# A gated mix of a long convolution and a dense block on one core: first weights and six first-layer blocks moved into the FFT phase, one record buffer for the power tables

## The chip, the core and the metric

The kernel runs on one core of one Trainium2 chip. The metric is device time in microseconds for one execution; the median of 11 runs is given. A page of the profile and a trace come from one further execution, and its own time stands beside its span below. TensorE multiplies matrices, VectorE (DVE in the profile) and ScalarE (ACT) do elementwise work, GpSimd (POOL) mostly issues DMAs here, and SyncE (SP) only issues DMAs.

## The reference

Sequence length L = 2048, width D = 448, state N = 256, hidden width F = 1792, all in bfloat16. The forward part is a gate between two blocks:

```
g = sigmoid((x * gate_w).sum(-1))
dt = exp(log_dt); dB = dt * (B_re + 1j B_im); C = C_re + 1j C_im
P[d,n,l] = exp(dt * (A_re + 1j A_im) * l)          # l rounded to bfloat16
K[d,l]   = real(sum_n C[d,n] P[d,n,l] dB[d,n])
a = irfft(rfft(u, 2L) * rfft(K, 2L))[:L] + u * Dskip
b = relu(x2 @ w1 + b1)**2 @ w2 + b2
out = g * a + (1 - g) * b
```

The function returns `out` and the gradients to all inputs but the dense block's input (14 of them) for a given `grad_out`. Both are computed in one program.

## The kernel before, in words

A Python program writes out the instructions, and a planner puts them in a fixed order for each engine: it works with its own costs, starts each instruction where its operands and engine are free, and keeps the program's order as the priority. `tc.issue_after(x)` tells it not to issue something ahead of x. Each engine then runs its list strictly in order, so an instruction that waits holds up everything behind it on that engine. The same holds for the DMA issues, which stand in the lists of SP, ScalarE and GpSimd. On-chip buffers are tiles with a tag (U16, R32, F17, P14, K28, S25, D16, ...): a new tile of a tag takes the memory of the old one, and what writes it waits for the last readers of that part of the memory. The profile shows a tile by the letter of its tag: R is R32, F is F17, P is P14, S is S25, U is U16, D is D16, K is K28.

**The FFT phase.** A convolution of length 4096 is done as two-stage FFTs on TensorE (`fwd1`, L230; `fwd2`, L258), through scratch in memory. `fwd1` on u and on DA (grad_out times g) fills gd; `spectrum(w, q)` (L664) reads a quarter q of gd back, runs `fwd2`, and stores the spectrum. The products of the two spectra (`cprod`, L281) and the first inverse stage (`inv1p`, L295, evacuated by L207, L208 and L217) give hd[0], which holds the gradient DK to the convolution kernel before its last stage; the eight stores of hd are issued by ScalarE (L299). `transposed` (L493, copies L496, stores L498) puts u and DB (grad_out times 1 - g) into memory in transposed form, as UT_d and DBT_d, in four blocks of 512 positions each, by way of three buffers in tag S25.

**The power tables.** The convolution kernel needs powers of exp(dt A). They are kept in 14 chunks of 32 channels each. `powers(gr)` (L625 to L655) makes the records of four chunks (the fourth group has two): the seeds (L640 to L644), then 11 levels. A level copies the current powers into the record (L648, ScalarE), squares them (L651, ScalarE), multiplies real by imaginary part (L652, VectorE) and subtracts the squares (L653, VectorE); the result is the next level's input. Then GpSimd stores the record of 1,920 KB (960 for the last) to rec_d (L655). There are two sets of buffers, `psets` (L609): a record buffer, two buffers that the powers alternate between (`cur`), and one for the squares. Set 0 has its record in tag F17 (F), its powers in R32 and its squares in W0, which is tag P14; set 1 has all three in R32 (R). The groups alternate between the sets. The program calls `powers(0)` after spectrum(0, 0), `powers(1)` after spectrum(1, 0), and `powers(2)` and `powers(3)` in the first two rounds of the loop over q.

**DK's way through memory.** hd[0] is loaded in four quarters, of which two go to tag D16 (D) and two to tag P14 (P); each is loaded in two halves, one issued by ScalarE and one by SP (`load_hs`, L322). TensorE sums them with constants (L721), ScalarE copies the sums (L725 to L727), they are stored to dk_d on both the SP and the GpSimd queue (L734), and come back in another form (L741, L743) to the top of tag K28 (DK). The weights w1 of the first dense layer are loaded by SP into tag U16 (L705, L708) and two UT blocks by GpSimd (`load_ut`, L576) into tag S25 in the same stretch. The loads of w2 (tag D16, L1037) are held back with `issue_after(lry1)` until the load of the second part of chunk 1's record (`load_ry`).

**The chunk loop.** For each chunk c, `load_rx` and `load_ry` bring the record (L806, L810), `expand_x` and `expand_y` (ScalarE, L815 to L822) spread it into tag F17, VectorE starts the tables (`seeds_x`, L802) and doubles them (`build_x`, L781 to L785; `build_y`, L792 to L795). TensorE makes the kernel rows from them (`kgen`, L852; `k_out`, L860) and transposes them (L878, L890; the transposes are copied by L879 and L891, or done by DMA, L898). For the gradient, `dk_chunk` (L903, L904) prepares DK, `back_z` multiplies (L921, copied by L925 on ScalarE), `back_p` multiplies by the tables on VectorE (L941) and sums on TensorE (L950). The back part of chunk c - 1 runs beside the build of chunk c.

**The dense block, woven into the chunk loop.** `hidden(lb, jp)` (L592, L595, then relu L597 and square L599 or L602 on ScalarE, and a store to rT_d, L603) makes two of the 14 first-layer tiles for block lb of 512 positions. It uses the UT block in S25, w1 in U16, writes the squares to S25 and the relu to a small ring. The six blocks hidden(0, 0) to hidden(0, 5) are called behind round c = 0 of the chunk loop (L1012 to L1014), with the PSUM banks X and S. All other dense work is called behind the loop, and the planner fills it into the loop's gaps: `project` (L1029) with the second weights, transposes of the weights (L1053, L1064), `row_block` (L1092 to L1105) for the gradient to the hidden layer.

**After the loop.** The finished kernel K is stored (L866), loaded in positions (`X<-k_d`, L1121 and L1124), and goes through `fwd1` (L230) and the FFTs for the output and the gradient to u. The weight gradients (L1178) follow from rT_d and dhT_d, which are loaded in rows (L1167).

Of the kernel before, what the change touches and what calls it, by code (L numbers as in the profile page):

```python
# [19 lines left out]
P = 128  # L20
L, D, N, F = 2048, 448, 256, 1792
LT = L // P
FT = F // P
DT = 4
# [9 lines left out]
RS = 1920  # L34
# [303 lines left out]
def kernel(ctx, tc, A_u, A_A_re, A_A_im, A_B_re, A_B_im, A_C_re, A_C_im, A_log_dt, A_Dskip,  # L338
# [3 lines left out]
    nc = tc.nc  # L342
    V, S, G_, T_ = nc.vector, nc.scalar, nc.gpsimd, nc.tensor
# [26 lines left out]
    K = Ker(tc, pool, psum)  # L370
# [66 lines left out]
    RA = K.t("R32", [P, 16384])  # L437
# [43 lines left out]
    SB = K.t("S25", [P, 12800])  # L481
# [93 lines left out]
    def load_ut(lb):  # L575
        G_.dma_start(UTb[lb % 2].rearrange("p a l -> p (a l)"), bass.AP(tensor=UT_d, offset=lb * P * 2048, ap=[[2048, P], [1, 2048]]))  # L576
# [29 lines left out]


    Fp = K.t("F17", [P, 8704])
    psets = [(Fp[:, 0:4 * RS], RA[:, 14336:16384], W0[:, 3584:4608]), (RA[:, 0:4 * RS], RA[:, 7680:9728], RA[:, 9728:10752])]  # L609

    def fields(r):

# [12 lines left out]
    def powers(gr):  # L625
        nch = min(4, NCH - 4 * gr)
        cs_ = slice(4 * gr, 4 * gr + nch)
        n = nch * W2
        rb, cb, qb = psets[gr % 2]
        R = rb.rearrange("p (c r) -> p c r", c=4)[:, 0:nch]  # L630
        xs, ys, lx, ly = fields(R)
        cur = [cb[:, 1024 * i:1024 * i + 1024].bitcast(fp32) for i in range(2)]
        sqr = qb.bitcast(fp32)

        def halves(ap):
            return ap[:, 0:2 * n].rearrange("p (t c w) -> p t c w", t=2, w=W2)
        lam = Lam[:, :, cs_]
        va = cur[1][:, 0:2 * n].rearrange("p (c t w) -> p c t w", t=2, w=W2)
        ua = cur[0][:, 0:2 * n].rearrange("p (c t w) -> p c t w", t=2, w=W2)
        S.copy(xs[:, :, :, :, 1], Wt[:, cs_])  # L640
        V.tensor_tensor(out=ua, in0=Wt[:, cs_], in1=lam[:, 0].unsqueeze(2).to_broadcast([P, nch, 2, W2]), op=ALU.mult)
        V.tensor_tensor(out=va, in0=Wt[:, cs_], in1=lam[:, 1].unsqueeze(2).to_broadcast([P, nch, 2, W2]), op=ALU.mult)
        V.tensor_tensor(out=xs[:, :, 0, :, 3], in0=ua[:, :, 0], in1=va[:, :, 1], op=ALU.subtract)
        V.tensor_tensor(out=xs[:, :, 1, :, 3], in0=ua[:, :, 1], in1=va[:, :, 0], op=ALU.add)  # L644
        x, y = lam, halves(cur[0])
        for k in range(NLEV):
            dst = xs[..., 2] if k == 0 else ys[..., 1] if k == 2 else lx[..., (1, 8, 9, 10).index(k)] if k in (1, 8, 9, 10) else ly[..., k - 3]
            S.copy(dst.rearrange("p c t w -> p t c w"), x)  # L648
            if k < NLEV - 1:
                sq = halves(sqr)  # L650
                S.activation(sq, x, ACT.Square)  # L651
                V.scalar_tensor_tensor(out=y[:, 1], in0=x[:, 0], scalar=2.0, in1=x[:, 1], op0=ALU.mult, op1=ALU.mult)  # L652
                V.tensor_tensor(out=y[:, 0], in0=sq[:, 0], in1=sq[:, 1], op=ALU.subtract)  # L653
                x, y = y, halves(cur[1 - k % 2])
        G_.dma_start(bass.AP(tensor=rec_d, offset=4 * gr * P * RS, ap=[[RS, P], [P * RS, nch], [1, RS]]), R)  # L655


    spw = K.t("K28", [P, 4, 4, 2, D])
    Pct = K.t("U16", [P, 8192])
    K.MIn = Pct[:, 7168:7296]  # L660
    K.st_more = [SB[:, 1792 * i:1792 * i + 1792].rearrange("p (a d) -> p a d", d=D) for i in range(2)]
    S.mul(K.MIn, K.MI[:, P:2 * P], -1.0)
    prd = [b.rearrange("p (i a d) -> p i a d", i=4, d=D) for b in (Pct[:, 0:3584], Pct[:, 3584:7168], RA[:, 10752:14336])]

    def spectrum(w, q):
        sp = spw[:, 2 * (q % 2) + w]
# [11 lines left out]
    for q in range(4):  # L678
        if q < 3:
            if q > 0:  # L680
                spectrum(0, q + 1)
            ls1 = spectrum(1, q + 1) or ls1
        for h in range(2):
            pr = prd[(2 * q + h) % 3]
            K.cprod(pr, spw[:, 2 * (q % 2) + 1], spw[:, 2 * (q % 2)], h)
            K.inv1p(pr, 2 * q + h, hd[0])
        if q == 0:
            with tc.issue_after(f10.ins):
                transposed(DB, DBT_d, (S.copy, V.tensor_copy))
        if q < 2:  # L690
            powers(q + 2)
    with tc.issue_after(ls1.ins):
        nc.sync.dma_start(bass.AP(tensor=DB_d, offset=0, ap=[[LT * D, P], [1, LT * D]]), flat(DB))
        load_const("Ew", nc.sync)
        NW2 = 32 * len(ekeys) - 4096
        Ew2 = SB[:, 10752:10752 + NW2]
        nc.sync.dma_start(Ew2, nc.inline_tensor(cs["Ew2"].astype(ml_dtypes.bfloat16), name="c_Ew2").ap())
    hsD, hsP = K.t("D16", [P, 8192]), K.t("P14", [P, 7168])
    hss = [b[:, 3584 * i:3584 * i + 3584].rearrange("p (g x d) -> p g x d", g=4, x=2) for b in (hsD, hsP) for i in range(2)]
    for q in range(4):  # L700
        lhs = K.load_hs(hd[0], q, hss[q], True)
    w1v = K.t("U16", [P, 8192])
    w1w = w1v[:, 0:7168].rearrange("p (a f) -> p a f", a=DT)
    with tc.issue_after(lhs.ins):
        nc.sync.dma_start(w1w[:, 0:3], bass.AP(tensor=B_w1.tensor, offset=B_w1.offset, ap=[[F, P], [P * F, 3], [1, F]]))  # L705
    for h in range(2):
        with tc.issue_after(lhs.ins):
            nc.sync.dma_start(w1w[64 * h:64 * h + 64, 3], bass.AP(tensor=B_w1.tensor, offset=B_w1.offset + 384 * F, ap=[[F, 64], [1, F]]))  # L708
    KB = K.t("K28", [P, 14336])
    DK = KB[:, 0:VA * D].rearrange("p (a d) -> p a d", d=D)  # L710
    G_.memset(KB[:, 12 * D:VA * D].bitcast(fp32), 0.0)
# [25 lines left out]
    for cpy in range(2):  # L737
        qe = (nc.sync, G_)[cpy]
        with tc.issue_after(ldk[cpy].ins):
            for (a0, na, r0, st_, _) in pieces:  # L740
                qe.dma_start(DK[64 * cpy:64 * cpy + 64, a0:a0 + na].rearrange("p a d -> p (a d)"),  # L741
                             bass.AP(tensor=dk_d, offset=r0 * D, ap=[[na * D, 64], [1, na * D]]))
            qe.dma_start(DK[64 * cpy:64 * cpy + 1, 12], bass.AP(tensor=dk_d, offset=768 * D, ap=[[D, 1], [1, D]]))  # L743

# [4 lines left out]
    XWs = [XB[:, 4096 * k:4096 * k + 4096].rearrange("p (t w a r) -> p t w a r", t=2, w=W2, a=NA) for k in range(2)]  # L749
    for k in range(2):  # L750
        mx = G_.memset(XB[:, 4096 * k:4096 * k + 4096].bitcast(fp32).rearrange("p (x n) -> p x n", n=NA)[:, :, VA:NA], 0.0)
    with tc.issue_after(mx.ins):
        load_ut(0)
        load_ut(1)
    Fv = K.t("F17", [P, 8704])
    Vt = Fv[:, 0:4096]
    PRY = Fv[:, 4096:5376].rearrange("p (l w t d) -> p l w t d", l=5, t=2, d=2)
# [215 lines left out]
    for c in range(NCH + 1):  # L973
# [15 lines left out]
        for half in range(2):  # L989
# [19 lines left out]
            ap = None  # L1009
            if c > 0:  # L1010
                ap = back_p(c - 1, XTs[c - 1][half], (z01, z23)[half], (2 * half, 2 * half + 1), ay if c < NCH else None)
        if c == 0:  # L1012
            for jp in range(6):
                hidden(0, jp, NT[4:6], [w1v[:, 7168:8192], Fv[:, 2048:3072], Fv[:, 3072:4096]])  # L1014

    ring = [w1v[:, 7168:8192], Fv[:, 2048:3072], Fv[:, 3072:4096], P2[:, 0:1024], P2[:, 1024:2048]]
    ni = 0
# [15 lines left out]

    w2v = K.t("D16", [P, 8192])
    w2n = w2v[:, 0:FT * D].rearrange("p (j d) -> p j d", d=D)
    with tc.issue_after(lry1.ins):
        G_.dma_start(w2n, bass.AP(tensor=B_w2.tensor, offset=B_w2.offset, ap=[[D, P], [P * D, FT], [1, D]]))  # L1037
    hidden(0, 6, NT[0:3], ring)
    for lb in range(4):
# [433 lines left out]
```

## Time and profile before

| what | value |
|---|---|
| median of 11 runs | 927.29 us (920.89 to 939.61) |
| the profiled execution | 917.96 us, span of the trace 916.2 us |
| TensorE busy (matmul) | 705.4 us, 77% |
| VectorE busy | 671.4 us, 73% |
| ScalarE busy | 577.5 us, 63% |
| GpSimd busy | 198.5 us, 22% |
| mean granted TensorE clock | 0.838 of full speed |
| DMA | 184.97 MB, mean 202 GB/s |

The span covers the instructions of one execution; all positions in us are counted from its start. A busy share is an average over the whole span, and the stages differ: from 60 to 90 us VectorE is busy 29.32 of 30 us, from 182 to 200 us TensorE is busy 2.67 of 18 us, from 228 to 252 us VectorE is busy 8.94 of 24 us and ScalarE 22.63.

How to read a row of the timeline: the start and the duration in us, the engine, the line of the kernel, the operation, the tile written and the tile read with their shapes, how many instructions were merged, and in square brackets how long the engine was idle before it and what ended that. SPq, ACTq and POOLq are the engines' own instruction queues; a DMA issued from there is not done when the row ends. A list of DMA issues gives the KB of one and the median us from issue to landing. In the chain of waits a row is only a start, a duration and what it was. A row by stretch gives the busy times of PE, PEld, DVE, ACT and POOL in that stretch with the number of instructions, then the TensorE clock, the DMA share and GB/s.

### The profile page before, as it was taken

How to read it: one execution, taken by the hardware profiler on the slowest of the kernel's cores; microseconds unless marked ns; L12 is line 12 of the kernel's file. 1: busy time of each engine (PE TensorE's matmuls, PEld its weight loads, DVE VectorE, ACT ScalarE, POOL GpSimd, SP SyncE). 2: the span in 40 equal slices, each digit the busy share in tenths (PEclk: the TensorE clock that was granted, in tenths of full speed). 3: DMA queues.
4: the chain of work that ended last, by engine and by line, in shares of the span. 5: the costliest groups of instructions: out<-in, count | busy, mean ns of one | idle time of the engine just before them, and what ended most of it. 6: DMA issues, size and time to landing. Idle time of an engine off the chain costs nothing.

```text
span 916.2 us, 18868 instructions
## 1 busy us (share of the span) xinstructions
PE 705.4 (77%) x7585; PEld 334.6 (37%) x7585; DVE 671.4 (73%) x1164; ACT 577.5 (63%) x915; POOL 198.5 (22%) x347
## 2 busy tenths in 40 slices
PE   3637676636978988788888988889859949989895
PEld 1212222224344443344444443444323315543352
DVE  4649968697399999999987899963418959759200
ACT  4537757716997879788687666565516634654543
POOL 2321000113202112121202311223213013354220
PEclk9755555658879899999967999999979879998998
DMA  8997395897536765457652965649999988789861
GB/s 202 350 186 269 121 363 235 305 307 221 138 69 130 151 141 126 101 120 161 152 128 68 235 157 158 143 141 258 322 410 270 303 259 248 219 228 276 187 163 54
DMA packets 169823, 184.97 MB, mean 202 GB/s; under 512 B 100531, under 2 KB 146904, under 8 KB 168808
## 3 DMA queue, kind: packets, MB, share of 16 engines
q1 hardware_dynamic: 118710, 81.48, 37.1%
q0 software_dynamic: 21344, 67.46, 22.4%
q10 hardware_dynamic: 29682, 34.84, 12.0%
q8 instruction: 59, 0.97, 0.4%
q14 instruction: 28, 0.23, 0.1%
HBM read 88.22 MB, written 73.13 MB: 176 GB/s over the span
## 4 chain that ended last, share of the span: by engine, by line
DVE 31%; PE 26%; ACT 14%; DMA 14%; issue 8%; SPq 3%; POOL 2%; ACTq 1%; POOLq 0%; DVEq 0%
PE psF L1178 5%; DVE F L793 4%; DVE P L941 4%; DMA hd<-st 3%; SPq L459 2%; PE psN L1029 2%; DVE Y L795 2%; DVE K L795 2%; DVE X L781 2%; DVE K L792 2%; DVE Y L792 2%; DVE F L782 2%; PE psN L1178 2%; DVE X L785 2%; DMA S<-rT_d 1%
## 5 line engine op out<-in xcount | busy, mean ns | idle before, releaser
L941 DVE TENSOR_TENSOR P<-R 128x2048 bf16<-128x2048 bf16 x42 | 49.5, 1218 | 25.2 <-ACT R L925 21.8
L925 ACT CAST R<-psF 128x1024 bf16<-128x1024 f32 x56 | 57.3, 1024 | 11.3 <-PE psF L921 11.2
L1178 PEld LDWEIGHTS <-S 128*128 128x128 bf16 x448 | 41.9, 100 | 53.6 <-issue 11.5
L1029 PE MATMUL psN<-D,S 128*128 128x448 bf16 x208 | 50.6, 374 | 6.3 <-ACT S L599 6.3
L1178 PE MATMUL psF<-U,S 128*128 128x448 bf16 x224 | 50.2, 370 | 2.9 <-ACT S L1173 2.8
L592 PE MATMUL psN<-S,U 128*128 128x512 bf16 x132 | 41.0, 429 | 8.2 <-ACT F L597 4.8
L921 PE MATMUL psF<-R,S 64*32 64x256 bf16 (+1 forms) x1344 | 36.8, 288 | 9.4 <-DMA R<-Y 3.6
L208 DVE CAST K<-psN 128x448 bf16<-128x448 f32 x36 | 22.0, 621 | 28.3 <-PE psN L258 28.1
L1092 PE MATMUL psN<-S,U 128*128 128x512 bf16 x126 | 36.2, 405 | 6.9 <-ACT D L1097 6.9
L781 DVE TENSOR_TENSOR X<-X,F 128x512 bf16<-128x512 bf16 (+1 forms) x70 | 37.5, 535 | 4.9 <-ACT F L815 3.1
L1105 POOL DMA_DIRECT2D dhT_d<-D x28 | 20.2, 721 | 91.4 <-DVE D L1104 91.0
L793 DVE TENSOR_TENSOR F<-K,F 128x2048 bf16<-128x2048 bf16 (+3 forms) x42 | 35.9, 854 | 3.7 <-ACT F L822 3.7
L258 PEld LDWEIGHTS <-M 128*64 128x64 bf16 x192 | 14.4, 133 | 64.7 <-issue 61.9
L792 DVE TENSOR_TENSOR K<-K,F 128x2048 bf16<-128x2048 bf16 (+3 forms) x42 | 36.4, 866 | 1.7
L782 DVE TENSOR_TENSOR F<-X,F 128x512 bf16<-128x512 bf16 (+1 forms) x70 | 37.0, 528 | 0.7 <-ACT F L816 0.2
L792 DVE TENSOR_TENSOR Y<-Y,F 128x2048 bf16<-128x2048 bf16 (+3 forms) x42 | 36.3, 864 | 1.6
L795 DVE TENSOR_TENSOR K<-K,F 128x2048 bf16<-128x2048 bf16 (+3 forms) x42 | 36.4, 866 | 1.3
L795 DVE TENSOR_TENSOR Y<-Y,F 128x2048 bf16<-128x2048 bf16 (+3 forms) x42 | 36.3, 865 | 1.3
L793 DVE TENSOR_TENSOR F<-Y,F 128x2048 bf16<-128x2048 bf16 (+3 forms) x42 | 35.9, 854 | 0.3 <-ACT F L822 0.3
L1029 PE MATMUL psN<-S,D 128*128 128x448 bf16 x168 | 35.7, 361 | 0.0
L921 PEld LDWEIGHTS <-S 64*16 64x16 bf16 (+1 forms) x1792 | 21.9, 89 | 33.3 <-issue 26.5
L891 ACT COPY M<-psX 128x1024 bf16<-128x1024 bf16 x26 | 26.5, 1019 | 11.7 <-PE psX L890 11.5
(407 smaller groups left out, 1939.2 us busy)
## 6 DMA issues: line engine op xcount, KB each, us to landing
sp<-K ACTq DMA_DIRECT2D x8, 896.0 KB, 4.1
hd<-st ACTq DMA_DIRECT2D x16, 448.0 KB, 5.1
dhT_d<-D POOLq DMA_DIRECT2D x28, 256.0 KB, 5.2
R<-sp SPq DMA_DIRECT2D x8, 896.0 KB, 25.6
S<-rT_d POOLq DMA_DIRECT2D x14, 512.0 KB, 6.6
R<-hd SPq DMA_DIRECT2D x16, 448.0 KB, 8.6
rec_d<-F POOLq DMA_DIRECT2D x2, 1920.0 KB, 8.0
Y<-gd SPq DMA_DIRECT2D x4, 896.0 KB, 10.6
```

Of the source, the lines that this page charges most:

```text
L592: T_.matmul(ps[:], lhsT=w1w[:, dt, j * P:j * P + P], rhs=ub[:, dt], start=(dt == 0), stop=False, skip_group_check=True)
L781: V.tensor_tensor(out=hi4, in0=lo, in1=bcast_dims(pr, [0, (None, n), 1]), op=ALU.mult)
L782: V.tensor_tensor(out=Vv.rearrange("p (x a r) -> p x a r", x=2 * W2, r=2), in0=lo, in1=bcast_dims(pi, [0, (None, n), 1]), op=ALU.mult)
L792: V.tensor_tensor(out=hi, in0=lo, in1=bcast_dims(pr, [0, (None, n // 2), 1]), op=ALU.mult)
L793: V.tensor_tensor(out=Vv.rearrange("p (x a q) -> p x a q", x=rows, q=2), in0=lo, in1=bcast_dims(pi, [0, (None, n // 2), 1]), op=ALU.mult)
L795: return V.tensor_tensor(out=T4[:, :, :, n:2 * n], in0=T4[:, :, :, n:2 * n], in1=V4, op=ALU.add)
L921: T_.matmul(psz[32 * ii:32 * ii + m, t, 256 * s:256 * s + 256], lhsT=DKc[64 * t:64 * t + 64, s, g, 2 * ii:2 * ii + 1 + par].rearrange("p i ...
L925: S.copy(zb[:, :, :, gg].rearrange("p s t n -> p t s n"), psz[:].rearrange("p t (s n) -> p t s n", s=2))
L941: lastp = V.tensor_tensor(out=pr.rearrange("p s t g n -> p s t (g n)"), in0=zv, in1=(xb if r == 0 else rev_dim(xb, 2)), op=ALU.mult)
L1029: lastm = T_.matmul(ps[:, 0:D], lhsT=hblk[j][:, P * tt:P * tt + P], rhs=ws[:, j, :], start=(w == 1 and j == 0), stop=(j == FT - 1))
L1092: T_.matmul(ps[:], lhsT=w2Tw[:, jp, dt, j % 2], rhs=dblk[:, dt], start=(dt == 0), stop=False, skip_group_check=True)
L1178: lastm = T_.matmul(ps[:, 0:width], lhsT=hh[:, t, :], rhs=(DB2[:, t, :] if w == 0 else U[:, t, 0:D + 1]), start=(t == 0), stop=(t == LT - 1))
```

## The change

The second record buffer is gone: all four tables use set 0, so the record is always in tag F17, the powers in R32, the squares in P14. The memory in R32 that this frees takes two of the three product buffers (`prd`) and the additional staging buffers of `inv1p` (`st_more`), which lay in U16 and S25; the negated constant `MIn` moves from U16 to F17. So U16 is free for w1 and the lower part of S25 for two UT blocks while the FFT phase still runs: their loads are now issued by GpSimd in round q = 0, behind the transposes of DB. The six calls hidden(0, 0) to hidden(0, 5) move from round c = 0 of the chunk loop to the end of the FFT phase, ahead of the loads of hd, with a ring of two buffers in place of three. Last, the load of w2 stands behind the last reload of DK (`lrl`) and no longer behind `lry1`. The arithmetic is the same.

Below line 660 the changed program's line numbers differ by a few: the hidden lines stay L592 to L603, L668 becomes L669, the lines of the hd sums L721 to L743 become L723 to L745, the lines of the chunk loop from L802 on are one less (L781 becomes L780, L815 becomes L814, L941 becomes L940), and those of the dense block from L1029 on are four less (L1025). The load of w1 is at L691 and L693, that of w2 at L1033.

```diff
-    psets = [(Fp[:, 0:4 * RS], RA[:, 14336:16384], W0[:, 3584:4608]), (RA[:, 0:4 * RS], RA[:, 7680:9728], RA[:, 9728:10752])]
+    psets = [(Fp[:, 0:4 * RS], RA[:, 14336:16384], W0[:, 3584:4608])]
...
-        rb, cb, qb = psets[gr % 2]
+        rb, cb, qb = psets[0]
...
-    Pct = K.t("U16", [P, 8192])
-    K.MIn = Pct[:, 7168:7296]
-    K.st_more = [SB[:, 1792 * i:1792 * i + 1792].rearrange("p (a d) -> p a d", d=D) for i in range(2)]
+    w1v = K.t("U16", [P, 8192])
+    w1w = w1v[:, 0:7168].rearrange("p (a f) -> p a f", a=DT)
+    K.MIn = Fp[:, 7680:7808]
+    K.st_more = [RA[:, 7168 + 1792 * i:8960 + 1792 * i].rearrange("p (a d) -> p a d", d=D) for i in range(2)]
     S.mul(K.MIn, K.MI[:, P:2 * P], -1.0)
-    prd = [b.rearrange("p (i a d) -> p i a d", i=4, d=D) for b in (Pct[:, 0:3584], Pct[:, 3584:7168], RA[:, 10752:14336])]
+    prd = [b.rearrange("p (i a d) -> p i a d", i=4, d=D) for b in (RA[:, 0:3584], RA[:, 3584:7168], RA[:, 10752:14336])]
...
         if q == 0:
             with tc.issue_after(f10.ins):
                 transposed(DB, DBT_d, (S.copy, V.tensor_copy))
+            G_.dma_start(w1w[:, 0:3], bass.AP(tensor=B_w1.tensor, offset=B_w1.offset, ap=[[F, P], [P * F, 3], [1, F]]))
+            for h in range(2):
+                G_.dma_start(w1w[64 * h:64 * h + 64, 3], bass.AP(tensor=B_w1.tensor, offset=B_w1.offset + 384 * F, ap=[[F, 64], [1, F]]))
+            load_ut(0)
+            load_ut(1)
         if q < 2:
             powers(q + 2)
...
+    for jp in range(6):
+        hidden(0, jp, NT[4:6], [w1v[:, 7168:8192], SB[:, 11776:12800]])
     hsD, hsP = K.t("D16", [P, 8192]), K.t("P14", [P, 7168])
...
     for q in range(4):
         lhs = K.load_hs(hd[0], q, hss[q], True)
-    w1v = K.t("U16", [P, 8192])
-    w1w = w1v[:, 0:7168].rearrange("p (a f) -> p a f", a=DT)
-    with tc.issue_after(lhs.ins):
-        nc.sync.dma_start(w1w[:, 0:3], bass.AP(tensor=B_w1.tensor, offset=B_w1.offset, ap=[[F, P], [P * F, 3], [1, F]]))
-    for h in range(2):
-        with tc.issue_after(lhs.ins):
-            nc.sync.dma_start(w1w[64 * h:64 * h + 64, 3], bass.AP(tensor=B_w1.tensor, offset=B_w1.offset + 384 * F, ap=[[F, 64], [1, F]]))
...
-                qe.dma_start(DK[64 * cpy:64 * cpy + 64, a0:a0 + na].rearrange("p a d -> p (a d)"),
+                lrl = qe.dma_start(DK[64 * cpy:64 * cpy + 64, a0:a0 + na].rearrange("p a d -> p (a d)"),
...
-    with tc.issue_after(mx.ins):
-        load_ut(0)
-        load_ut(1)
...
-        if c == 0:
-            for jp in range(6):
-                hidden(0, jp, NT[4:6], [w1v[:, 7168:8192], Fv[:, 2048:3072], Fv[:, 3072:4096]])
...
-    with tc.issue_after(lry1.ins):
+    with tc.issue_after(lrl.ins):
         G_.dma_start(w2n, bass.AP(tensor=B_w2.tensor, offset=B_w2.offset, ap=[[D, P], [P * D, FT], [1, D]]))
```

More of the change, by code (lines that the diff above doesn't have):

```diff
@@ L697 @@
         nc.sync.dma_start(Ew2, nc.inline_tensor(cs["Ew2"].astype(ml_dtypes.bfloat16), name="c_Ew2").ap())
+    assert NW2 <= 1024
+    for jp in range(6):
+        hidden(0, jp, NT[4:6], [w1v[:, 7168:8192], SB[:, 11776:12800]])
     hsD, hsP = K.t("D16", [P, 8192]), K.t("P14", [P, 7168])
```

## The prediction

> **What bounds the kernel now.** I read the page first (span 916.2 us in an execution of 917.96 us), then its chain of waits, then the timeline of the stretch that the change touches (60 to 260 us), engine by engine. The chain has four pieces: the FFT phase to 182 us, the way of DK through memory and back to 226 us, a knot of ScalarE and TensorE work to 253 us, and then the chunk loop on VectorE to 607 us.
>
> The FFT phase holds the four power tables. Each ends with a store of its record, issued by GpSimd (GpSimd's timeline, then the list of DMA issues: KB, us from issue to landing):
>
> ```profile
> 113.38 0.79 POOL L655 DMA_DIRECT2D rec_d<-F  x1 [32.49 <-DVE R L653]
> 134.92 0.77 POOL L655 DMA_DIRECT2D rec_d<-R  x1 [17.66 <-ACT R L648]
> 162.92 0.77 POOL L655 DMA_DIRECT2D rec_d<-F  x1 [19.30 <-ACT F L648]
> 179.57 0.73 POOL L655 DMA_DIRECT2D rec_d<-R  x1 [0.78 <-ACT R L648]
> ```
>
> ```profile
> rec_d<-F POOLq DMA_DIRECT2D x2, 1920.0 KB, 8.0
> rec_d<-R POOLq DMA_DIRECT2D x1, 960.0 KB, 5.2
> ```
>
> F and R take turns: while one record is stored, the next table is already being made in the other. Table 1 ran beside table 0 (its first VectorE step at 93 us, table 0's last ScalarE copy at 112 us). The timeline of ScalarE shows the pace inside a table: one level is a copy and a square on ScalarE and two steps on VectorE:
>
> ```profile
> 155.92 0.62 ACT L648 CAST F<-R 128x512 bf16<-128x512 f32 x1 [1.34 <-DVE R L653]
> ...
> 157.56 0.62 ACT L648 CAST F<-R 128x512 bf16<-128x512 f32 x1 [0.49 <-DVE R L653]
> ```
>
> So a level undisturbed costs 1.64 us (157.56 - 155.92), ten of them 16.4; for the half table 3 the same lines are 1.08 us apart. Then VectorE starts the chunk loop, and stops once for long (timeline, all engines):
>
> ```profile
> 182.72 0.42 DVE L781 TENSOR_TENSOR X<-X,F 128x512 bf16<-128x512 bf16 x1 [2.07 <-ACT F L815]
> ...
> 226.31 0.89 ACT L903 COPY S<-K 128x416 bf16<-128x416 bf16 x1 [5.23 <-DMA K<-dk_d]
> ...
> 245.10 2.36 DVE L941 TENSOR_TENSOR P<-R 128x2048 bf16<-128x2048 bf16 x2 [14.09 <-ACT R L925]
> ...
> 253.51 2.36 DVE L941 TENSOR_TENSOR P<-R 128x2048 bf16<-128x2048 bf16 x2 [1.78 <-ACT R L925]
> ```
>
> ```profile
> 282.00:392.00 110.00, 93.53 (x1513) 46.43 (x1512) 106.98 (x156) 92.37 (x130) 21.75 (x36) 0.95 0.60 129
> ```
>
> The reader sees the tables of chunks 0 and 1 built from 182.7 to 231.0, then 14.09 us of nothing: the z copies (L925) stand on ScalarE among the six hidden blocks. L903 is the first use of the reloaded DK. The last line is a row of busy times by stretch (PE, PEld, DVE, ACT, POOL): from 282 to 392 VectorE is busy 106.98 of 110 us. From there a delay of VectorE is not won back; a chunk takes 27.7 us.
>
> **The change part by part.**
>
> *Hidden blocks out of the knot.* Twelve L597 (0.69 to 0.76 us) and six L599 (1.06 to 1.15) are about 15 us of ScalarE between 234 and 252. Gone from there, they free VectorE of at most the waits above: 14.09 + 1.78, with the smaller ones before (1.03, 1.45, 2.29) 20.6 us. In the FFT phase their ScalarE time falls into the gaps of tables 2 and 3 (ScalarE waits 0.49 us per level there); I charge 2 us each.
>
> *Weights.* The first weights (1.3 + 0.4 MB) and two UT loads move from 187 to 212 us on SP's and GpSimd's queues to about 70 to 95 on GpSimd's, where DMA is busy 0.46 to 0.70. The second weights leave GpSimd's queue ahead of the dk_d stores (issued 204.07) and go behind the reloads. dk_d then needs some 5 us instead of the chain's 10.07, if DK still sets the pace.
>
> *One record buffer.* This is the cost. Table n+1 may not write F, and by the changed order neither engine passes that point, until record n has landed; the shared scratch would not let the levels overlap either. In the changed program's order all of table 1 stands behind table 0 on ScalarE and VectorE. Behind each wait stand the last FFT copies and hidden activations; these have slack. Two things have none. expand_x(0) writes tag F17, so it waits until record 3 has landed; before, F was free with record 2 (162.92 + 8.0) and it ran at 171.5. And the loads of the second half of hd go to tag P14, where the scratch of every table now lies: they are issued behind table 3's last step on ScalarE and SP; before, table 3 used R.
>
> The serial sum, from rows of before:
> - Table 0 ends at 114. VectorE's order from L559 on holds some 30 us of steps from about 81; stalls 3. Bounds 109 and 118 (before: 112.8).
> - Landing: 0.8 issue + 8.0 + 0.2 = 9: 123.
> - Table 1: start-up 2.7 (L640, first L648) + 16.4 + 1.6 (two wider copies) = 21 bare; table 2 of before, from 135.18 to 162.6 with as many FFT steps between and 5 us of waits for transposes, 27. I take 25: 148.
> - Landing 9, and 1.5 for the X memsets that stand ahead of this store on GpSimd's queue and wait for TensorE: 158.5.
> - Table 2: 21 bare, with hidden activations 22.5 (to 26): 181. Landing 9.5 beside the hd loads: 190.5.
> - Table 3: 13 bare, 16.7 in before (162.53 to 179.3); I take 15.5: 206. Landing 5.2 + 0.8 + 0.2: 212.
> - The first L814 takes 0.63: VectorE starts chunk 0 at **213**, 30 us after 182.72. All low ends together give 201, all high ends 224.
>
> The page "DMA: Bandwidth & Descriptors" of the Trainium skill (section on the anatomy of a SWDGE DMA) puts a DMA from GpSimd at about 2.0 us plus bytes over 436 GB/s, an estimated 6.5 us for a record of 1.97 MB. The rows say 8.0. By the page three landings would be 1.5 us shorter each and the whole sum about 4.5 us lower. "Trainium Kernel Development and Optimization" (Best Practices) says to double-buffer so that DMA and compute overlap; this change takes a double buffer away, and the rows price it.
>
> *The loop.* From 182.72 to the end of the second L941 pair (255.87) are 73.2 us; less 20.9 of idle time, 52.3 of work. Then 213 + 52.3 + 1 = 266.3, **+10.4**. DK: the hd loads at 206, landed at 215 (8.5 us), last Ew product 219, copies 221, dk_d 226, reload 9 as before (217.24 to 226.3): 234 or 235; then the copies on ScalarE (L902 to L924, 22 us of steps): z is there at 256 to 257, VectorE at 257. A near tie; I add 1.5.
>
> *One chunk of dense work ahead.* In the changed order TensorE has done 392 project products and all of row blocks 0 to 2 when the last chunk's kernel product is done; before 336. The pattern of slow chunks (31.3, 34.7, 32.6, 30.7 us between L802 lines) moves one chunk forward, and one plain chunk of 27.7 becomes a filled one of about 29: +1.3. After the loop 50 L1029 and 9 L1092 (621 to 636, about 15 us) are no longer there. But fwd1 (L230, at 635.46) also waits for X<-k_d, whose loads are issued until 633.0 and would land at about 632 at best: I take 3 us, and 2.5 for eight products fewer in row block 3: **-5.5**, bounds 0 and -12.
>
> Sum: 10.4 + 1.5 + 1.3 - 5.5 = +7.7 us on 917.96. The median of eleven runs is 927.29, 1% above the profiled one; I carry the same difference over: **935 us**. Ends: with 201 for 213 and -12: about -20; with 224 and 0: +26; not all at once.
>
> **Rivals.**
> *Faster.* The FFT steps no longer share their engines with two tables at a time, each table runs near its bare pace, and the 14 us stall is gone. It decides at a start of chunk 0 before 205 us (where the sum above is zero). For it: bare 21 us, an FFT phase with DVE busy 20.25 of 30 us from 120 to 150. Against: three landings of 9 us with nothing in them for the tables. At 201 the sum is 12 less: -4, and with the page's landings somewhat more: 922 us.
> *DK's way becomes the bound.* TensorE's order puts a product that needs the second weights (L1025) ahead of chunk 0's transposes and kernel product. Those weights, issued at about 231 behind the reloads, took 13.0 us to land in before: 244, some 4 us late, and with the high ends for table 3 and the landings, 5 us more, the z copies fall to 266, 9 us behind VectorE: 935 - 1.5 + 9, 942 us and more.
> *Nothing to be seen.* The loop ends 10 us late, but the 15 us of TensorE work that was moved ahead is the bound after it, and it comes back whole: +13 - 12 is about 928.
>
> **How the numbers follow.** The forecast (930 to 941) 0.50, DK's way (941 to 955) 0.15, nothing 0.16, faster 0.19. A measurement tells 0.3%, about 2.8 us, from no change. So slower 0.65, same 0.16, faster 0.19. The range 922 to 947 leaves out about half of the faster case and half of the DK case.
>
> **What would show it.** Record stores at about 115, 149, 181 and 206 with nothing of the next table before the landing; the first L780 at 213; VectorE almost idle from 185 to 213; no long wait before the first L940 at 257; L230 some 5 us later than 635. The steps are wrong if the fourth record store comes before 198, if L780 starts without it, or if VectorE waits over 5 us before L940. Then the time is a rival's.

## The result, and the profile after

The changed kernel takes 940.08 us (median of 12 runs, 929.28 to 944.69); the kernel before takes 927.64 (median of 47, 919.63 to 939.61). The ratio is **1.0113, 95% interval 1.0081 to 1.0145**: some 10 us slower. The ratio leaves out three of the twelve runs that lie over 1.5% above the fastest; the median holds them. The forecast was 935 (+7.7), in the range 922 to 947. The profiled execution took 937.57 us with a span of 935.8, 19.6 us more than the span of before; the profile of before (917.96) lies 1% under its own median, the profile of after 0.3% under its own. So differences between the two traces are some 7 us larger than those between medians.

GpSimd's timeline of after, where the four record stores answer to those shown of before (start, duration, idle time before it):

```profile
123.69 0.78 POOL L655 DMA_DIRECT2D rec_d<-F  x1 [16.48 <-DVE R L641]
155.46 0.77 POOL L655 DMA_DIRECT2D rec_d<-F  x1 [0.63 <-ACT F L648]
188.42 0.77 POOL L655 DMA_DIRECT2D rec_d<-F  x1 [3.44 <-ACT F L648]
211.83 0.72 POOL L655 DMA_DIRECT2D rec_d<-F  x1 [4.36 <-ACT F L648]
```

All from F, the last 32 us later than in before (179.57). The list of DMA issues shows that the short record lands slower than in before (5.2):

```profile
rec_d<-F POOLq DMA_DIRECT2D x3, 1920.0 KB, 7.5
rec_d<-F POOLq DMA_DIRECT2D x1, 960.0 KB, 10.9
```

VectorE's timeline of after: the first steps of tables 2 and 3, the first step of chunk 0, the first product of the back part:

```profile
168.28 0.73 DVE L643 TENSOR_TENSOR F<-R 128x256 bf16<-128x256 f32 x1 [3.87 <-DMA rec_d<-F]
...
195.69 0.44 DVE L643 TENSOR_TENSOR F<-R 128x128 bf16<-128x128 f32 x1 [7.12 <-DMA rec_d<-F]
...
224.53 0.43 DVE L780 TENSOR_TENSOR X<-X,F 128x512 bf16<-128x512 bf16 x1 [13.44 <-ACT F L814]
...
267.31 2.35 DVE P L940 x2
```

The first three waits end with a landing, the third by way of L814, which is expand_x(0). The last line is from the chain of waits: L940 has no long wait ahead of it any more, where L941 had 14.09 us in before. ScalarE's timeline shows L814 behind the second half of the hd loads, which ScalarE and SP issue within 1 us of record 3's store:

```profile
211.13 1.43 ACTq L322 DMA_DIRECT2D P<-hd  x2
222.83 0.63 ACT L814 ACTIVATE F<-recx 128x512 bf16<-128x512 bf16 x1 [11.30 <-DMA rec_d<-F]
```

Record 3 has two chunks and lies in columns 0 to 3840 of F17, while expand_x writes columns 6656 to 8704 (L758 and L759 of the changed kernel). Record 2 did reach there, but it had landed by 195.6 us, when table 3 began to write the record buffer. So, as far as the kernel and the trace tell, this wait is not for the part of the memory that is written, as said of the tags above, but for the last user of the old tile as a whole. No run keeps record 3 in F17 without this wait. The rows by stretch show the hole and the loop (columns as in before):

```profile
282.00:392.00 110.00, 93.77 (x1461) 45.50 (x1454) 106.32 (x153) 88.83 (x126) 22.31 (x37) 0.91 0.61 130
182.00:230.00 48.00, 26.56 (x196) 9.74 (x195) 15.10 (x43) 29.63 (x57) 7.64 (x12) 0.71 0.60 172
```

From 182 to 230 us VectorE is busy 15.10 of 48 us (40.45 in before); from 282 to 392 it is as full as before (106.98). Where the 19.6 us of the two spans come and go, by landmarks that both traces have:

| landmark | before | after | difference |
|---|---|---|---|
| first step of chunk 0 (L781, L780) | 182.72 | 224.53 | +41.8 |
| end of the second pair of products (L941, L940) | 255.87 | 275.46 | +19.6 |
| seeds of the last chunk (L802, L801) | 578.72 | 605.35 | +26.6 |
| first L230 after the loop | 635.46 | 656.22 | +20.8 |
| end | 916.2 | 935.8 | +19.6 |

### The profile page after: what moved, and what is told of

It is laid out like the page before. It is cut to its first block, busy times and chain, and to the rows that moved or that the text cites. A ratio compares the mean times of both kernels' runs of the same rounds, so it can differ in the third digit from the quotient of the medians.

```text
span 935.8 us, 18881 instructions
## 1 busy us (share of the span) xinstructions
PE 727.4 (78%) x7585; PEld 339.9 (36%) x7585; DVE 671.1 (72%) x1164; ACT 578.4 (62%) x915; POOL 198.1 (21%) x346
## 4 chain that ended last, share of the span: by engine, by line
PE 28%; DVE 17%; ACT 15%; DMA 14%; issue 11%; POOL 1%; ACTq 1%; SPq 0%; POOLq 0%; DVEq 0%
PE psF L1174 4%; PE psN L1025 4%; DMA rec_d<-F 3%; DVE F L792 2%; ACT R L924 2%; PE psX L851 2%; DMA S<-rT_d 2%; DMA hd<-st 2%; DMA R<-Y 2%; PE psX L889 2%; PE psN L592 2%; PE psF L920 1%; DVE X L780 1%; DVE P L940 1%; DVE K L791 1%
## 5 line engine op out<-in xcount | busy, mean ns | idle before, releaser
L940 DVE TENSOR_TENSOR P<-R 128x2048 bf16<-128x2048 bf16 x42 | 49.7, 1218 | 10.5 <-ACT R L924 7.1
L1025 PE MATMUL psN<-D,S 128*128 128x448 bf16 x208 | 51.6, 381 | 6.7 <-ACT S L599 6.7
L1174 PE MATMUL psF<-U,S 128*128 128x448 bf16 x224 | 52.6, 383 | 3.2 <-ACT S L1169 3.1
L780 DVE TENSOR_TENSOR X<-X,F 128x512 bf16<-128x512 bf16 (+1 forms) x70 | 37.3, 533 | 15.2 <-ACT F L814 13.4
L592 PE MATMUL psN<-S,U 128*128 128x512 bf16 x132 | 39.9, 419 | 9.3 <-ACT F L597 4.2
L648 ACT CAST F<-R 128x512 bf16<-128x512 f32 (+1 forms) x40 | 25.0, 626 | 25.7 <-DVE R L653 25.6
L781 DVE TENSOR_TENSOR F<-X,F 128x512 bf16<-128x512 bf16 (+1 forms) x70 | 36.9, 527 | 0.6
L1025 PE MATMUL psN<-S,D 128*128 128x448 bf16 x168 | 37.0, 371 | 0.0
```

Of the source, the lines that this page charges most:

```text
L592: T_.matmul(ps[:], lhsT=w1w[:, dt, j * P:j * P + P], rhs=ub[:, dt], start=(dt == 0), stop=False, skip_group_check=True)
L780: V.tensor_tensor(out=hi4, in0=lo, in1=bcast_dims(pr, [0, (None, n), 1]), op=ALU.mult)
L781: V.tensor_tensor(out=Vv.rearrange("p (x a r) -> p x a r", x=2 * W2, r=2), in0=lo, in1=bcast_dims(pi, [0, (None, n), 1]), op=ALU.mult)
L940: lastp = V.tensor_tensor(out=pr.rearrange("p s t g n -> p s t (g n)"), in0=zv, in1=(xb if r == 0 else rev_dim(xb, 2)), op=ALU.mult)
L1025: lastm = T_.matmul(ps[:, 0:D], lhsT=hblk[j][:, P * tt:P * tt + P], rhs=ws[:, j, :], start=(w == 1 and j == 0), stop=(j == FT - 1))
L1174: lastm = T_.matmul(ps[:, 0:width], lhsT=hh[:, t, :], rhs=(DB2[:, t, :] if w == 0 else U[:, t, 0:D + 1]), start=(t == 0), stop=(t == LT - 1))
```

## The experiments

Two theories stood against each other. **A:** the one buffer is the loss; the tables run one behind the other with a landing between, and chunk 0 begins late. **B:** the moved work is the loss: the six blocks ahead of the loop, the weights, the dense work that is one chunk ahead. Ratios are to the kernel before, run on the same chip; line numbers are each kernel's own. "Start" is the first step of chunk 0, "product" the first L941 or its counterpart, "seeds" those of the last chunk, "L230" the first after the loop. Every kernel is planned anew, so an edit can also move instructions that it does not name.

**One buffer alone.** The kernel before, with the first edit of the change only:

```diff
-    psets = [(Fp[:, 0:4 * RS], RA[:, 14336:16384], W0[:, 3584:4608]), (RA[:, 0:4 * RS], RA[:, 7680:9728], RA[:, 9728:10752])]
+    psets = [(Fp[:, 0:4 * RS], RA[:, 14336:16384], W0[:, 3584:4608])]
...
-        rb, cb, qb = psets[gr % 2]
+        rb, cb, qb = psets[0]
```

> The kernel before with one edit: all four tables use set 0, nothing else moves. Theory (the table chain on one buffer costs the time): record stores near those of the changed kernel (123, 155, 188, 212 us, perhaps 5 to 10 us sooner because no hidden blocks stand between the levels), first step of chunk 0 (L781) at 210 to 222 instead of 182.7, and 8 to 18 us more than before (ratio 1.009 to 1.020). Rival (the time is lost by the moved hidden blocks and weights): within 3 us of before (0.997 to 1.003).

Measured: 1.0274 (1.0206 to 1.0341), some 25 us. Record stores at 123, 157, 184, 207, start at 220.1. Theory A's mechanism and place are right, and B alone falls; but the loss is larger than I gave it, and more than twice the whole change. So the rest of the change wins some 15 us.

**Second weights late, alone.** The kernel before with `lrl` in place of `lry1`:

```diff
-                qe.dma_start(DK[64 * cpy:64 * cpy + 64, a0:a0 + na]...
+                lrl = qe.dma_start(DK[64 * cpy:64 * cpy + 64, a0:a0 + na]...
...
-    with tc.issue_after(lry1.ins):
+    with tc.issue_after(lrl.ins):
```

> The kernel before with only the load of the second weights behind the last reload of DK. Theory: no part of the loss; dk_d stores 2 to 4 us quicker, z copies a little earlier, within 3 us of before (0.996 to 1.003). Rival (DK's way and the second weights bound the start of the loop): 5 us or more slower (1.005 and up), with a wait for the second weights on TensorE's list before the first L941.

Measured: 0.9954 (0.9915 to 0.9993). The first use of the reloaded DK moves from 226.31 to 221.57 us and the product from 245.1 to 240.4: the whole 4.7 us reach VectorE. A gain of some 4 us, just past the better end of what I gave; my rival with the second weights on TensorE's list falls.

**Hidden blocks back behind round 0**, weights early, one buffer:

```diff
-    for jp in range(6):
-        hidden(0, jp, NT[4:6], [w1v[:, 7168:8192], SB[:, 11776:12800]])
...
+        if c == 0:
+            for jp in range(6):
+                hidden(0, jp, NT[4:6], [w1v[:, 7168:8192], Fv[:, 2048:3072], Fv[:, 3072:4096]])
```

> The changed kernel with the six hidden blocks back behind round 0 of the chunk loop; weights early, one buffer. Theory: the blocks cost the tables 3 to 8 us at most, so chunk 0 starts at 216 to 222 instead of 224.5, and the time stays 1.006 to 1.020 of before; the dense pattern goes back one chunk, so fwd1 (L230) starts no longer 6 us nearer to the end of the loop. Rival (the moved blocks are the loss): 0.998 to 1.004 of before.

Measured: 1.0215 (1.0141 to 1.0289), just above the range. Start 218.5 (6 us sooner than the changed kernel), seeds 599.1 (6 us sooner), but L230 at 660.8 (4.6 us later). The early blocks cost 6 us ahead of the loop, and more than that comes back behind it. Of the 14.5 us between the two spans, 9.9 lie behind L230 (289.5 us against 279.6, see the last section).

**Table 3 in its own memory** (product buffers of R32, free by then), called behind the FFT loop:

```diff
+    psets = [(Fp[:, 0:4 * RS], RA[:, 14336:16384], W0[:, 3584:4608])] * 3 + [(RA[:, 0:3840], RA[:, 3840:5888], RA[:, 5888:6912])]
...
-        if q < 2:
+        if q < 1:
             powers(q + 2)
+    ones(psets[3][0])
+    powers(3)
```

> The changed kernel, but table 3 is called behind the FFT loop and has its record, powers and squares in the memory of the product buffers (R32), so that it waits neither for the landing of record 2 nor stands between record 2 and expand_x in F17, and the second half of hd no longer waits for its squares. Theory: F17 is free with record 2, first step of chunk 0 at 196 to 205 instead of 224.5, second hd loads at 175 to 195, and the time falls to 0.985 to 1.000 of before, 12 to 25 us under the changed kernel. Rival (what comes behind the tables, DK and the dense work, sets the time): 1.006 or more of before although chunk 0 starts early.

Measured: 1.0109 (1.0023 to 1.0196): nothing won, against theory A. The last record is stored at 193.4, 18 us sooner than in the changed kernel, and table 3 ends on VectorE at 192. Yet the start is at 215.5 (VectorE's timeline of this kernel, then ScalarE's):

```profile
215.53 0.43 DVE L783 TENSOR_TENSOR X<-X,F 128x512 bf16<-128x512 bf16 x1 [23.62 <-ACT F L817]
```

```profile
198.06 0.69 ACT L597 ACTIVATE U<-psX,b_f 128x512 bf16<-128x512 f32 x1 [5.24 <-DMA rT_d<-U]
...
212.88 1.06 ACT L599 ACTIVATE S<-S 128x1024 bf16<-128x1024 bf16 x1
213.84 0.62 ACT L817 ACTIVATE F<-recx 128x512 bf16<-128x512 bf16 x1
```

L817 is expand_x(0). It no longer waits for any landing; it stands behind the six hidden blocks on ScalarE's list, and these take until 213.9 us: the ring has two buffers, so from the third on a block needs the store of the block two before it (5.24 us at the third here), and the later blocks wait 1.4 to 1.8 us each for TensorE. The blocks are a **second cover** over the start of chunk 0. I charged them 2 us each; in the changed kernel the record chain lay over them and hid this.

**Both: table 3 in its own memory and the blocks back behind round 0** (the two edits above together).

> Two edits to the changed kernel together: table 3 in its own memory, and the hidden blocks back behind round 0. Theory (in the kernel with table 3 alone moved, the six hidden blocks on ScalarE's list held expand_x until 213 us): with both, the first step of chunk 0 comes at 192 to 200, the DK reload at about 225, the first L940 at 243 to 252, and the time is 8 to 18 us below the kernel with only the hidden blocks moved back (1.003 to 1.013 of before). Rival (chunk 0 starts early, but TensorE's dense work sets the end in any case): the last chunk's seeds and the time as with only the hidden blocks moved back, 1.015 or more.

Measured: 1.0108 (1.0029 to 1.0187), against 1.0215 with the blocks moved back only: theory A in the ratio. The start is at 205.5 and not at 192 to 200 (ScalarE, then VectorE):

```profile
198.22 0.63 ACT L815 ACTIVATE F<-recx 128x512 bf16<-128x512 bf16 x1 [10.21 <-DMA rec_d<-F]
...
202.63 0.53 ACT L728 CAST st<-psN 128x448 bf16<-128x448 f32 x1 [3.17 <-PE psN L724]
```

```profile
199.50 0.29 DVE L654 TENSOR_TENSOR R<-R 128x128 f32<-128x128 f32 x1 [10.83 <-ACT R L652]
...
205.46 0.42 DVE L781 TENSOR_TENSOR X<-X,F 128x512 bf16<-128x512 bf16 x1 [0.23 <-ACT F L815]
```

expand_x(0) (L815) waited for record 2, which landed 13.8 us after its issue at 184.45, beside the hd loads. Here the planner put the last levels of table 3 behind it on ScalarE's list, with a copy of the DK sums (L728) among them, and on VectorE's list they stand ahead of the start. Start, product, seeds and L230 are 13.0, 11.5, 8.6 and 8.8 us sooner than with the blocks back alone: with the blocks in the knot, most of a sooner start reaches the end.

**Blocks filled in by the planner**, on the kernel before with late second weights:

```diff
-        if c == 0:
-            for jp in range(6):
-                hidden(0, jp, NT[4:6], [...])
...
-    hidden(0, 6, NT[0:3], ring)
+    for jp in range(7):
+        hidden(0, jp, NT[0:3], ring)
```

> The kernel before with the second weights behind DK's reloads, and the six hidden blocks called with the rest of the dense work behind the loop, in PSUM banks N0 to N2, so that the planner fills them into gaps. Theory (in before the z copies stand 5.6 us apart among hidden activations): the first L941 moves from 240 to 230 to 234 us, the wait ahead of it falls from 14.0 to 4 to 8 us, the loop ends 6 to 10 us sooner. If VectorE bounds the loop to its end, the time is 0.983 to 0.990 of before; if TensorE does (rival: the dense work put off comes back behind the loop), 0.995 to 1.005.

Measured: 0.9963 (0.9913 to 1.0012): the rival. The product comes at 233.2, 7 us sooner than with late second weights alone, and the wait ahead of it falls to 7.84 us, as the theory said; but the last seeds are 7 us later (582.5) and L230 10 us later (643.8). Dense work that is put off comes back in the loop and behind it.

**A second set for the tables, with all else of the change.** Nothing in the memory map is free, so this costs two product buffers in place of three and the additional staging buffers:

```diff
+    psets = [(Fp[:, 0:4 * RS], [SB[:, 11776:12800], w1v[:, 7168:8192]], W0[:, 3584:4608]),
+             (RA[:, 7168:14848], [SX[:, 7168:8192], SY[:, 7168:8192]], RA[:, 14848:15872])]
...
-    K.st_more = [...]
-    prd = [... for b in (RA[:, 0:3584], RA[:, 3584:7168], RA[:, 10752:14336])]
+    prd = [... for b in (RA[:, 0:3584], RA[:, 3584:7168])]
```

> The changed kernel with a second set for the tables: record and squares in R32, the powers in four unused tails of other tiles; in return two product buffers in place of three and no additional staging buffers for the inverse stage. Early weights and early hidden blocks stay. Theory (the single buffer is the loss): record stores within 8 us of those of before (113, 135, 163, 180), the hidden blocks still hold expand_x to 200 to 208, and the time is 0.985 to 0.998 of before, 13 us or more below the changed kernel. Rival (the early blocks are the loss): 1.005 or more.

Measured: 1.0026 (0.997 to 1.0082), between my two ranges: some 8 us below the changed kernel where I gave 13 or more, and level with before. The tables are back at their old times (117, 133, 163, 181), so the smaller buffers cost little there, and the start is still at 211.2, behind the hidden blocks, which end at 204.4, and behind a copy of the DK sums (L727) that waited 4.66 us for TensorE (VectorE, then ScalarE):

```profile
211.17 0.43 DVE L780 TENSOR_TENSOR X<-X,F 128x512 bf16<-128x512 bf16 x1 [26.65 <-ACT F L814]
```

```profile
199.35 0.69 ACT L597 ACTIVATE U<-psX,b_f 128x512 bf16<-128x512 f32 x1 [4.15 <-DMA rT_d<-U]
199.40 0.52 ACTq L322 DMA_DIRECT2D P<-hd  x1
...
203.33 1.06 ACT L599 ACTIVATE S<-S 128x1024 bf16<-128x1024 bf16 x1
209.04 0.53 ACT L727 CAST st<-psN 128x448 bf16<-128x448 f32 x1 [4.66 <-PE psN L723]
209.47 0.63 ACT L814 ACTIVATE F<-recx 128x512 bf16<-128x512 bf16 x1
```

The second line shows another thing that the blocks hold up: ScalarE's share of the loads of hd is issued from the same list, the last at 202.07 us. TensorE sums what these loads bring, and L727 waits for the sums.

**Two sets, blocks filled in** (both edits above).

> As the kernel with a second set of table buffers, but the hidden blocks called with the rest of the dense work behind the loop, in PSUM banks N0 to N2. Theory: chunk 0 starts at 183 to 190, DK is back by 220, the first L940 at 228 to 234, no wait over 6 us before it, time 0.978 to 0.990 of before. Rival (TensorE sets the end of the loop): the first L940 is as early, but the last seeds are not, and the time is 0.993 to 1.005.

Measured: 0.9914 (0.9873 to 0.9956), between the two cases. Start 183.8 and product 229.9 as the theory said, 15 us sooner than in before; last seeds only 5 us sooner (573.6), L230 not at all (635.2).

**Record stored in three pieces**, changed kernel otherwise:

```diff
+            if k == 7:
+                for a_, b_ in ((0, 512), (1024, RS)):
+                    G_.dma_start(bass.AP(tensor=rec_d, offset=4 * gr * P * RS + a_, ...), R[:, :, a_:b_])
...
-        G_.dma_start(... offset=4 * gr * P * RS, ...), R)
+        G_.dma_start(... offset=4 * gr * P * RS + 512, ...), R[:, :, 512:1024])
```

> The changed kernel with each record stored in three pieces: columns 0 to 512 and 1024 to 1920 after level 7, the rest (512 KB of 1,920) at the end. Theory: what the next table waits for is the landing of 512 KB, so the gaps between a table's end and the next table's start fall from 9.1, 12.8 and 7.3 us to 3 to 6 each and the last from 11 to 4 to 7; the first step of chunk 0 comes at 205 to 215 instead of 224.5, but not ahead of the hidden blocks (last L599 at about 205). Time 1.000 to 1.010 of before, since in kernels with early blocks an earlier start was given back in the loop. Rival (the landing is not what the tables wait for): record stores at the times of the changed kernel (155, 188, 212) and no gain.

Measured: 1.0114 (1.0069 to 1.0159), no gain, and just above my range. The landing is what the tables wait for: last pieces are stored at 121.8, 150.4, 176.3 and 199.1, the last 12.7 us sooner than the whole record of the changed kernel. The start is at 217.6, 7 us sooner but later than the 205 to 215 that I gave, and nothing of it is left at the last seeds (604.7 against 605.4). expand_x(0) began at 207.79, when record 3 had landed, and its second half stood behind a copy of the DK sums that waited 7.59 us for TensorE.

**Two sets, blocks behind the expansion of chunk 0's record**, that is behind it in the planner's priority:

```diff
     expand_x(0)
     expand_y(0)
+    for jp in range(6):
+        hidden(0, jp, NT[4:6], [w1v[:, 7168:8192], RT_[:, 15360:16384]])
```

> The kernel with a second set of table buffers and early weights; the six hidden blocks are called right behind the expansion of chunk 0's record and ahead of the chunk loop (the second ring buffer in R32). Theory (the blocks' place on ScalarE's list, ahead of expand_x and of the loads of hd, held chunk 0 to 211 us in the kernel with two sets): first step of chunk 0 at 183 to 190, first L940 at 232 to 240, the dense pattern stays one chunk ahead and fwd1 comes 50 to 53 us after the last seeds; time 0.983 to 0.997 of before. Rival (the loop with early blocks ends at about 604 us whatever the start): last seeds at 598 or later, 0.998 to 1.005.

Measured: **0.977 (0.9662 to 0.9879)**, 913.04 us, the fastest of all, faster than both kernels and better than the range I gave. There are only four runs of it, so the interval is wide. VectorE's timeline:

```profile
183.10 0.43 DVE L778 TENSOR_TENSOR X<-X,F 128x512 bf16<-128x512 bf16 x1 [2.07 <-ACT F L812]
...
241.40 2.36 DVE L938 TENSOR_TENSOR P<-R 128x2048 bf16<-128x2048 bf16 x2 [5.29 <-DMA R<-K]
```

Start as in before; the blocks fill ScalarE and TensorE from 190 to 227 us while DK is on its way (row of 182 to 230: TensorE busy 28.00, ScalarE 28.11, VectorE 39.37 us of 48). The product is a little later than I gave (two waits, 7.45 and 5.29 us), the last seeds are at 577.6, and L230 comes 49.2 us behind them, not 56.7 as in before.

**Two sets, blocks behind round 0.**

> The kernel with a second set of table buffers, early first weights and late second weights, hidden blocks behind round 0 as in before. Against the kernel with only the second weights late (0.995) it shows the first weights alone. Theory: the first weights no longer share the queues and DMA engines with DK's loads, DK is back 2 to 5 us sooner, the wait ahead of the first L941 stays at 11 to 15 us behind the blocks; 0.988 to 0.996 of before. Rival (fewer product and staging buffers cost as much in the FFT phase): 0.996 to 1.003.

Measured: 0.9891 (0.9837 to 0.9945). Against late second weights alone (0.9954) the first use of DK moves from 221.57 to 215.56 and the product from 240.4 to 234.7; the early first weights are worth some 6 us on the traces, with the smaller product buffers in it; the intervals of the two ratios overlap.

**One buffer, blocks behind the expansion** (the changed kernel with the last diff shown, that behind `expand_y(0)`).

> The changed kernel (one buffer for the tables) with only the six hidden blocks moved, right behind the expansion of chunk 0's record. Theory (two things hold chunk 0, each to 213 us or later: the chain of records and the blocks ahead of expand_x on ScalarE's list; taking away one leaves the other): tables as with the blocks behind round 0, first step of chunk 0 at 216 to 221, first L940 at 258 to 266, fwd1 50 to 53 us after the last seeds, time 1.002 to 1.013 of before, within 10 us of the changed kernel and 20 us or more behind the kernel with two sets and the blocks in this place (0.977). Rival (the place of the blocks is the whole loss): 0.995 or less of before.

Measured: 1.0208 (1.0131 to 1.0285). The rival falls: the place of the blocks alone wins nothing. The start is at 217.8, and what holds it is the record again (ScalarE's timeline):

```profile
216.14 0.63 ACT L812 ACTIVATE F<-recx 128x512 bf16<-128x512 bf16 x1 [11.28 <-DMA rec_d<-F]
```

But the time is above what theory A gave (1.002 to 1.013), some 9 us more than the changed kernel. The last seeds and L230 are at 606.6 and 657.0, within 1.3 us of the changed kernel's; most of the difference, 6.3 us of 7.1 between the two spans, arises in the loads and FFTs behind, which are nearly the same in both. There the granted TensorE clock is lower (0.85 against 0.88 in the 100 us that begin 60 us behind L230). Why is open.

Six of the kernels make a table (ratio, start):

| | blocks behind round 0 | ahead of expand_x | behind expand_x |
|---|---|---|---|
| one buffer | 1.0215, 218.5 us | 1.0113, 224.5 us (the change) | 1.0208, 217.8 us |
| two sets | 0.9891, 181.7 us | 1.0026, 211.2 us | 0.977, 183.1 us |

A second set, for all its smaller product buffers, is worth 30 us in the first column, 41 in the last, and only 8 in the one that the change stands in (27, 30 and 3 us on the traces by L230; the rest lies in the end of the program), since there the blocks hold chunk 0 whether the tables are done or not. Only with both covers gone does chunk 0 start at 183 us and the early blocks pay.

## Why the prediction was right, point by point

**Direction and place: right.** The loss is the one record buffer, by the landing between tables and the wait of expand_x(0) for record 3; the stores, the hole of VectorE, and the missing stall ahead of L940 came as told. One buffer alone (+25 us) and the second set (-8 to -41 us) show it. That the time lay in the range is in part luck, as the sum below shows.

**Table 0 at 114: wrong,** 123.7 by the issue of its store, outside my bounds of 109 and 118. Two copies of the transposed DB (L496) stand among its last four levels on VectorE's list and waited 3.52 us for TensorE and 2.96 for a landing; I had charged 3 us of stalls in all; VectorE's waits from 81 us to the end of the table add up to 10.7. One buffer alone has the same two waits (3.52 and 2.99 us) and its store at 123.33, so the delay comes with the one buffer and not with the moved work.

**Landings: 5 us more than I took.** I took 9, 10.5, 9.5 and 6.2; measured from issue to the next step are 9.1, 12.8, 7.3 and 11.0. Record 1's landed only after 12.7 us, and the last term was mis-sized: 960 KB took 10.9 us beside the second half of the hd loads, which I had waiting for table 3's last step myself, and whose traffic I did not put into this term. In before the same store took 5.2.

**Tables 1 to 3 at 25, 22.5 and 15.5:** 22.7, 20.1 and 16.1 measured, 4 us less in sum. With the 1.7 us from L814 to L780 these terms make 224.5 in place of 213, just past the top of my bounds (224).

**Hidden blocks at 2 us each, in the gaps of tables 2 and 3: the step that failed,** though it did not show in the time. Their ScalarE time does fall into gaps, but their place on the list does not: the blocks end at 208 us in the changed kernel, at 214 and 204 in the two kernels where the record chain is shorter or gone, and expand_x stands behind them (in the last also behind the copy of the DK sums, to 209). So my "faster" rival (a start before 205 us) could not have come about by faster tables; with tables done at 181 the start was at 211.

**The loop, +10.4 by the end of the second pair: +19.6,** by the 11.5 us of the start, less 2.4: the stretch took 50.9 us, not the 52.3 and 1 that I counted. **DK's tie, 1.5 us:** not there; DK was first used at 241.46, later than my 234, but VectorE was later still and lost no more than 1 us ahead of L940. The rival of DK's way falls for this kernel. **Dense pattern, +1.3: mis-sized,** +7.0 from the second pair to the last seeds. Six chunks take 30.5 to 32.8 us in the changed kernel where four took 30.6 to 34.7 in before: two more filled chunks, not one, and at some 32 us each, not 29. VectorE's waits for TensorE (view of waits: engine, line, releaser, us, times, longest) grow:

```profile
DVE P L940 <- PE psN L949: 8.0, 3, 4.6
```

against 3.7 us in before. In the kernel with two sets and the blocks ahead they are 16.0, and its lead of 13 us over the changed kernel at the product is 1.9 at the last seeds.

**After the loop, -5.5: right.** From the last seeds to L230 it took 56.7 us in before and 50.9 in the changed kernel. All six kernels with the blocks ahead of the loop have 49 to 51 us here, all eight others 57 to 62. "What would show it" had L230 some 5 us later than 635, less than its own sum of 7.7; it was 20.8, with the start.

**The sum** was 7.7 for 19.6 between the profiled executions, and 10 between the runs. It looks closer than it is: I carried the profile's distance from its median (1%) over to the changed kernel, whose profile was only 0.3% under its own. On the traces the sum was 12 us short, 9 in the loop's start and 6 in the dense pattern, against 3 in smaller terms.

## What to carry to other kernels

A step that starts late can have two covers: before pricing one wait, follow the engine's list back from the late step and ask what it would have waited for next; taking away one cover alone gave 8 us at best here, both together 32. An in-order list prices a moved block by where it stands, not by the idle time that it fits into: against their old place and with two sets, the same six blocks cost 13 us ahead of a critical instruction and won 11 behind it (7 us on the traces by L230; the two intervals overlap). With one buffer, where the record holds the start in any case, it was not so: 1.0113 ahead and 1.0208 behind. And a buffer that is given up to bring loads forward has to be set against the landing that it exposes each time it is reused, at the DMA load of that moment.

## What the runs showed of the hardware

Stores by GpSimd with the record's layout (list of DMA issues of the kernel with three pieces, KB and median us to landing):

```profile
rec_d<-F POOLq DMA_DIRECT2D x6, 512.0 KB, 3.8
...
rec_d<-F POOLq DMA_DIRECT2D x3, 896.0 KB, 5.0
```

384 KB more take 1.2 us. By an estimate from these two sizes, which are medians of stores in different traffic, some 2.2 us are fixed and the rest goes at about 330 GB/s; that makes 8.2 us for 1,920 KB, where the other kernels have medians of 6.8 to 8.5 us, and one of them 10.9 (table 3 in its own memory). The Trainium skill ("DMA: Bandwidth & Descriptors", the anatomy of a SWDGE DMA) has nearly the same fixed part, 2.0 us, and a higher rate, 436 GB/s. The spread by traffic is larger than this difference. 960 KB took 10.9 to 11.6 us in the four kernels that issue four loads of hd (448 KB each) within 1 us ahead of the store, and 4.3 to 5.2 in eight that do not (8.3 in the kernel with table 3 in its own memory). From 211.8 to 222.8 us of the changed kernel the DMA engines moved 256 GB/s, that is 2.8 MB, as much as the record and the four loads together.

The program from L230 to the end is nearly the same in all fourteen kernels (1,417 to 1,427 matrix instructions on TensorE in the records), but took 279.6 us (the changed kernel) to 289.5 (one buffer, blocks behind round 0) in the profiled executions. In the 100 us that begin 60 us behind L230, the granted TensorE clock is 0.90 in before, 0.88 in the changed kernel and 0.85 in the longest; over the 290 us from L230 it is 0.89, 0.89 and 0.87. Whether the clock accounts for the whole difference is not shown. The difference between two profiled executions is therefore uncertain by some 10 us in their end, and the landmarks inside the loop compare better than the spans.
